# Second MoE in blocks of 512 tokens, one w_in chunk a step, in place of blocks of 256 and two chunks

## The chip, the core and the metric

The kernel runs on one core of one Trainium2 chip. The metric is the device time of one execution in microseconds (us). PE is TensorE (its weight loads are shown apart, as PEld), DVE is VectorE, ACT is ScalarE, POOL is GpSimd and SP is SyncE, which here only issues DMAs.

## The reference

Sliding-window attention feeds a bilinear MoE, and its result feeds a second MoE with a rational activation. The second MoE is what the change touches:

```
x = attention(q, k, v)                    # (2304, 512) after the heads are put together
x = ((x @ w1) * (x @ w2)) @ w3 @ w_out    # first MoE: 512 -> 1024 -> 1024 -> 512
h = x @ w_in                              # second MoE: 512 -> 2048
P = a[0] + a[1]*h + a[2]*h**2 + a[3]*h**3
Q = 1.0 + abs(b[0])*abs(h) + abs(b[1])*h**2
out = (P / (Q + 1e-06)) @ w_out           # 2048 -> 512
```

Inputs are float64 words that the kernel turns into fp32. To keep accuracy each operand of the large products is held as a high and a low part in fp32r, and a product is three matmuls: high by high, high by low, low by high (`SPLIT`).

## The kernel before

Phase 1 runs attention and the first MoE by a planner that orders its jobs. The first MoE works on chunks of 288 tokens (`TA`); its last chunk is finished inside phase 2 by `tail(n)`, n from 0 to 3.

Phase 2 is written out by hand, and each engine runs its instructions in the written order. The 2304 tokens are nine blocks of `TB` = 256. The 16 chunks of 128 hidden units are taken in four groups (`g`) of four. A step is one block and two chunks, so that a step's hidden tile is 128 x 512; there are 4 x 9 x 2 = 72 steps. What one step i writes, in this order:

- `hmm(i)` on PE: the hidden tile by 24 matmuls of 256 columns (two chunks, three products, four pieces of the contraction), into one of four PSUM banks (tags ab and px).
- `ins(i)`: ACT makes |h| (tile v), y and t, POOL multiplies y by v (L782), DVE makes the numerator in the hidden bank (L784, L785).
- `l4(i-4)` on PE: the output product of the step four before, 12 matmuls of 512 columns (L819) into accumulator banks, one for each 128 tokens. There are four of these banks (tags acc and sc), and a block of 256 tokens uses two over its two steps of a group.
- `split_g(i-1)`: ACT casts the quotient to its high part (L807), POOL subtracts for the low part (L808).
- `seed(i)` on ACT: Ln and Exp of the denominator (L791, L792); L791 waits for POOL's L782.
- `evict`: when a block's last `l4` of a group is written, its accumulators are copied to SBUF (ACT, L830, in group 0) or added to it (DVE, L832, later).
- `quotient(i)` on DVE (L797, L799, L801), and `weights(i)`, the load and the split of the next weights.
- `x_split` after steps 3, 6 and 9: a block's input is split, the high part by DVE (L740), the low part by POOL (L742). Five blocks are loaded and split in phase 1 (`NX1`), three in phase 2, and the last comes from `tail`.

At the start of phase 2, `tail(0)`, step 0, `tail(1)`, step 1, `tail(2)`, step 2 and `tail(3)` alternate, then the first four chunks of the second MoE's w_out are split (`b_split`: ACT L244, then POOL or DVE L248), and then steps 3, 4 and so on follow. Step 4 is the first with an `l4`.

Of the kernel before, what the change touches and what calls it, by code (L numbers as in the profile page):

```python
# [10 lines left out]
F32 = mybir.dt.float32  # L11
F32R = mybir.dt.float32r
# [6 lines left out]
P = 128  # L19
B, H, S, D = 4, 8, 576, 64  # L20
HP = H // 2
NT = B * S
# [158 lines left out]
class Kern:  # L181
# [308 lines left out]
    def phase1(self):  # L490
# [189 lines left out]
        done.eng = "DVE"  # L680
        for blk in range(NX1):
            ks = range(blk * TB // TA, ((blk + 1) * TB - 1) // TA + 1)
            ld = add("SP", 1.7, self.x_load, blk, after=[done] + [stored[k, n] for k in ks for n in range(KC)],
                     due=end - 30 + 5 * blk)
            add("DVE", 1.95, self.x_split, blk, after=[ld], due=end - 25 + 5 * blk, port=True)
        for f in range(FG):
            db = buf("dec0")
            pb = buf(f"p{f}")
# [39 lines left out]

    def x_load(self, blk):

        n = TB if blk < NB - 2 else TL
        x = self.XS[blk][:, 1].bitcast(F32)
        self.nc.sync.dma_start(out=x[:, :, 0:n], in_=self.x2d[:, :, blk * TB:blk * TB + n].rearrange(
            "c p t -> p c t"))

    def x_split(self, blk, lo_pool=False):
        nc = self.nc
        n = TB if blk < NB - 2 else TL
        hi, lo = self.XS[blk][:, 0, :, 0:n], self.XS[blk][:, 1, :, 0:n]
        nc.vector.tensor_copy(hi, lo.bitcast(F32))  # L740
        eng = nc.gpsimd if lo_pool else nc.vector
        eng.tensor_tensor(out=lo, in0=lo.bitcast(F32), in1=hi.bitcast(F32), op=ALU.subtract)  # L742

    def phase2(self, X, wk):
        nc, XS = self.nc, self.XS
        steps = [(g, blk, h) for g in range(NG) for blk in range(NB) for h in range(FG // 2)]
        PG = NB * FG // 2
        N = len(steps)
        hps, tt, yy, rr, gt, acc, adds = {}, {}, {}, {}, {}, {}, []
        self.nh = self.na = 0  # L750

# [4 lines left out]
        def accbank():  # L756
            self.na += 1
            return self.bank(("acc", "acc", "sc", "sc")[(self.na - 1) % 4])

        def buf(tag, bufs):  # L760
            return wk[tag].tile([P, 2 * TB], F32, tag=tag, bufs=bufs, name=tag)

        def hmm(i):
            g, blk, h = steps[i]
            t = hps[i] = hbank()
            for e in range(2):
                w = self.win[g * FG + 2 * h + e]
                n = 0
                for s in SPLIT:
                    for c in range(KC):  # L770
                        nc.tensor.matmul(t[:, e * TB:(e + 1) * TB], w[:, s[0], c * P:(c + 1) * P],  # L771
                                         XS[blk][:, s[1], c], start=n == 0, stop=n == 11)
                        n += 1

# [27 lines left out]
                                           op1=ALU.mult, reverse0=True)  # L802

        def split_g(i):
            u = tt.pop(i).rearrange("p (e t) -> p e t", e=2)
            t = gt[i] = self.gp.tile([P, 2, 2, TB], F32R, tag="g", bufs=5, name="gg")
            nc.scalar.copy(t[:, 0], u)  # L807
            nc.gpsimd.tensor_tensor(out=t[:, 1], in0=u, in1=t[:, 0].bitcast(F32), op=ALU.subtract)  # L808

        def l4(i):  # L810
            g, blk, h = steps[i]
            t = gt.pop(i)
            if h == 0:
                acc[g, blk] = [accbank() for _ in range(TB // P)]
            for e in range(2):
                w = self.wo2[g * FG + 2 * h + e]
                for tk in range(TB // P):
                    for s in SPLIT:
                        nc.tensor.matmul(acc[g, blk][tk], t[:, s[0], e, tk * P:(tk + 1) * P],  # L819
                                         w[:, s[1]], start=(h, e) == (0, 0) and s == (0, 0),  # L820
                                         stop=(h, e) == (FG // 2 - 1, 1) and s == (1, 0))
            if h == FG // 2 - 1:
                adds.extend((g, blk, tk) for tk in range(TB // P))

        def evict(on_act):
            if adds and on_act == (adds[0][0] == 0):
                g, blk, tk = adds.pop(0)
                a, x = acc[g, blk][tk], X[blk][:, tk * DM:(tk + 1) * DM]
                if g == 0:
                    nc.scalar.copy(x, a)  # L830
                else:
                    nc.vector.tensor_tensor(out=x, in0=a, in1=x, op=ALU.add)  # L832
                if g == NG - 1:
                    r = blk * TB + tk * P
                    nc.sync.dma_start(out=self.out[r:r + P, :], in_=x)

        def weights(i):
# [14 lines left out]
        def step(i):  # L852
            if i < N:
                hmm(i)
                ins(i)
            if i >= LAG:
                l4(i - LAG)
            if 1 <= i <= N:
                split_g(i - 1)
            if i < N:  # L860
                seed(i)
            evict(False)
            if i < N:
                quotient(i)
                weights(i)
            evict(False)
            evict(True)
            evict(True)
            for blk, k in X_SPLIT:
                if i == k:  # L870
                    self.x_split(blk, True)

        def tail(n):

            for e in range(2):
                self.l2(NA - 1, n, e)
            d = TA - TB
# [7 lines left out]
        for blk, _ in X_SPLIT:  # L885
            self.x_load(blk)
        for f in range(2):
            self.b_load(1, f)
# [11 lines left out]
    def run(self):  # L900
        with self.pool("cpool") as self.cpool, self.pool("decp") as self.decp, \
# [6 lines left out]

            def new_x(pool, blks):
                for n in blks:  # L910
                    self.XS[n] = pool.tile([P, 2, KC, TB], F32R, name=f"XS{n}")

# [6 lines left out]
            def attention_done():  # L919
                over.close()  # L920
                wk["r"] = right.enter_context(self.pool("b3", side="right"))
                new_x(wk["r"], range(NX1))

            self.attention_done = attention_done
            with self.pool("Q") as self.Q, self.pool("xs23") as self.xs23, self.pool("tp") as self.tp:
# [1 line left out]
                    self.phase1()  # L927
            with self.pool("b1") as b1:
                for n in range(NB):
                    X[n] = b1.tile([P, KC * TB], F32, name=f"X{n}")  # L930
                new_x(b1, range(NB - 1, NX1 - 1, -1))
# [61 lines left out]
```

## Time and profile before

| | us |
|---|---|
| median of 3 runs | 880.43 |
| lowest and highest | 877.05, 881.59 |
| the profiled execution, its time | 881.49 |
| the profiled execution, its span | 879.72 |

The span is the time from the first to the last instruction. The profile is of one execution, and the trace's times are counted from the span's start. Phase 2 takes the stretch from about 460 us to the end.

### The profile page before, as it was taken

How to read it: one execution, taken by the hardware profiler on the slowest of the kernel's cores; microseconds unless marked ns; L12 is line 12 of the kernel's file. 1: busy time of each engine (PE TensorE's matmuls, PEld its weight loads, DVE VectorE, ACT ScalarE, POOL GpSimd, SP SyncE). 2: the span in 40 equal slices, each digit the busy share in tenths (PEclk: the TensorE clock that was granted, in tenths of full speed). 3: DMA queues.
4: the chain of work that ended last, by engine and by line, in shares of the span. 5: the costliest groups of instructions: out<-in, count | busy, mean ns of one | idle time of the engine just before them, and what ended most of it. 6: DMA issues, size and time to landing. Idle time of an engine off the chain costs nothing.

```text
span 879.7 us, 16149 instructions
## 1 busy us (share of the span) xinstructions
PE 850.3 (97%) x5984; PEld 759.7 (86%) x5984; DVE 584.6 (66%) x1275; ACT 540.5 (61%) x1240; POOL 338.3 (38%) x316
## 2 busy tenths in 40 slices
PE   6989798999999999999999999999999999999998
PEld 3546598999998999989999889999999999999996
DVE  6999996677764212326125567779878877797775
ACT  5874564555465424542235578989877777787663
POOL 2220031332223221312122566676655655564442
PEclk9999999899999999999999999999999999999999
DMA  9776337576652202013111100010000100000112
GB/s 363 285 275 229 128 132 241 181 235 229 239 192 86 73 2 73 19 53 96 55 52 63 49 13 25 13 37 25 25 13 25 37 13 13 13 25 37 48 48 85
DMA packets 37710, 84.54 MB, mean 96 GB/s; under 512 B 4096, under 2 KB 11776, under 8 KB 37632
## 3 DMA queue, kind: packets, MB, share of 16 engines
q1 hardware_dynamic: 37632, 83.51, 27.8%
q8 instruction: 47, 0.77, 0.4%
q14 instruction: 31, 0.25, 0.1%
HBM read 66.26 MB, written 17.24 MB: 95 GB/s over the span
## 4 chain that ended last, share of the span: by engine, by line
PE 77%; DVE 7%; DMA 6%; ACT 5%; issue 3%; POOL 1%; SPq 0%; POOLq 0%; DVEq 0%; ACTq 0%
PE ab L437 20%; PE sc L819 11%; PE px L771 10%; PE acc L819 10%; PE ab L771 10%; PE acc L467 9%; DMA words<-moe_w_in 2%; PE sc L319 2%; PE px L384 2%; DMA words<-moe_w 2%; PE acc L417 2%; PE px L369 1%; DVE dec L226 1%; DMA qT<-q 1%; PE ab L417 1%
## 5 line engine op out<-in xcount | busy, mean ns | idle before, releaser
L437 PE MATMUL ab<-xs,w 128*128 128x288 f32 x1536 | 218.6, 302 | 6.1 <-ACT a_sb L443 2.7
L437 PEld LDWEIGHTS ab<-xs,w 128*128 128x128 f32 x1536 | 209.6, 191 | 12.3 <-ACT w L244 3.3
L782 POOL TENSOR_TENSOR y<-y,v 128x512 f32<-128x512 f32 x72 | 95.2, 1322 | 145.8 <-ACT y L781 144.0
L459 POOL TENSOR_TENSOR pp<-p,pp 128x288 fp32r<-128x288 f32 x64 | 54.0, 845 | 196.2 <-ACT pp L454 193.2
L362 POOL TENSOR_TENSOR pr<-pr,sm 96x384 f32<-96x384 f32 x64 | 55.2, 880 | 151.4 <-DVE sm L353 106.9
L467 PE MATMUL acc<-pp,w 128*128 128x288 f32 x768 | 111.2, 299 | 0.0
L771 PEld LDWEIGHTS px<-XS,w 128*128 128x128 f32 x864 | 106.8, 190 | 2.7 <-issue 0.2
L771 PEld LDWEIGHTS ab<-XS,w 128*128 128x128 f32 x864 | 106.9, 190 | 2.6
L771 PE MATMUL px<-XS,w 128*128 128x256 f32 x864 | 107.8, 281 | 0.0
L771 PE MATMUL ab<-XS,w 128*128 128x256 f32 x864 | 107.8, 281 | 0.0
L819 PE MATMUL acc<-w,gg 128*128 128x512 f32 x432 | 104.9, 391 | 1.4 <-POOL w L248 0.8
L819 PE MATMUL sc<-w,gg 128*128 128x512 f32 x432 | 104.7, 391 | 1.0 <-ACT X L830 1.0
L467 PEld LDWEIGHTS acc<-pp,w 128*128 128x128 f32 x768 | 103.5, 188 | 2.3
L808 POOL TENSOR_TENSOR gg<-t,gg 128x512 fp32r<-128x512 f32 x72 | 93.4, 1297 | 5.8 <-ACT gg L807 5.1
L819 PEld LDWEIGHTS acc<-w,gg 128*128 128x128 f32 x432 | 78.8, 188 | 16.9 <-POOL w L248 1.2
L819 PEld LDWEIGHTS sc<-w,gg 128*128 128x128 f32 x432 | 78.8, 188 | 16.3 <-ACT X L830 1.2
L346 ACT ACTIVATE pr<-pr,sm 96x128 f32<-96x128 f32 x192 | 74.7, 391 | 22.3 <-DVE sm L340 21.2
L447 DVE TENSOR_TENSOR p<-a_sb,ab 128x288 f32<-128x288 f32 x64 | 29.0, 452 | 88.7 <-PE ab L437 80.6
L799 DVE SCALAR_TENSOR_TENSOR v<-y,cs,r 128x512 f32<-128x512 f32 x72 | 77.1, 1071 | 0.0
L791 ACT ACTIVATE r<-y,cs 128x512 f32<-128x512 f32 x72 | 52.3, 727 | 27.2 <-POOL y L782 27.2
L218 ACT ACTIVATE dec<-words 128x512 f32<-128x512 f32 x72 | 47.6, 674 | 33.6 <-DMA words<-moe_w_in 11.3
L454 ACT CAST pp<-p 128x288 fp32r<-128x288 f32 x64 | 27.6, 432 | 56.1 <-DVE p L447 56.0
(77 smaller groups left out, 1199.4 us busy)
## 6 DMA issues: line engine op xcount, KB each, us to landing
words<-moe_w SPq DMA_DIRECT2D x32, 512.0 KB, 5.4
words<-moe_w_out SPq DMA_DIRECT2D x24, 512.0 KB, 4.5
words<-moe_w_in SPq DMA_DIRECT2D x16, 512.0 KB, 4.0
wd<-dec SPq DMA_DIRECT2D x32, 256.0 KB, 2.3
c<-wd SPq DMA_DIRECT2D x32, 256.0 KB, 2.7
vb<-v SPq DMA_DIRECT2D x16, 384.0 KB, 3.5
kT<-k SPq DMA_DIRECT2D x16, 304.0 KB, 4.7
qT<-q SPq DMA_DIRECT2D x16, 288.0 KB, 5.3
```

What stands on the lines that cost most here:

```text
L218: self.nc.scalar.activation(out=d.bitcast(F32), in_=s["words"].bitcast(F32)[:, :, 1], func=AF.Copy, scale=2.0 ** -112)
L346: self.nc.scalar.activation(out=pr[:, i], in_=pr[:, i], func=AF.Exp, scale=0.125, bias=sm[:, 1, i:i + 1], accum_out=sm[:, 2, i:i + 1])
L362: nc.gpsimd.tensor_tensor(out=pr[:, i], in0=pr[:, i], op=ALU.mult, in1=sm[:, 3, i].unsqueeze(2).to_broadcast([QT, 3, P]))
L437: self.nc.tensor.matmul(t[:, 0:TA], w[:, s[0], c * P:(c + 1) * P], xs[:, s[1], c], start=n == 0, stop=n == 11)
L459: eng.tensor_tensor(out=w[:, 1], in0=p, in1=w[:, 0].bitcast(F32), op=ALU.subtract)
L467: self.nc.tensor.matmul(acc[:, 0:TA], self.W3o[m][0][:, a, n * P:(n + 1) * P], self.p2[k, m // 2][:, c, m % 2], start=m == 0 and (a, c) == ...
L771: nc.tensor.matmul(t[:, e * TB:(e + 1) * TB], w[:, s[0], c * P:(c + 1) * P], XS[blk][:, s[1], c], start=n == 0, stop=n == 11)
L782: nc.gpsimd.tensor_tensor(out=w, in0=w, in1=v, op=ALU.mult)
L791: nc.scalar.activation(out=r, in_=yy[i][1], func=AF.Ln, bias=self.c1)
L799: nc.vector.scalar_tensor_tensor(out=v, in0=w, scalar=self.c1, in1=r, op0=ALU.add, op1=ALU.mult)
L808: nc.gpsimd.tensor_tensor(out=t[:, 1], in0=u, in1=t[:, 0].bitcast(F32), op=ALU.subtract)
L819: nc.tensor.matmul(acc[g, blk][tk], t[:, s[0], e, tk * P:(tk + 1) * P], w[:, s[1]], start=(h, e) == (0, 0) and s == (0, 0), stop=(h, e) == ...
```

## The change

`TB` becomes 512: four blocks of 512 tokens and one of 256 (`BLK`). In a block of 512 a step takes one chunk, so that the hidden tile is again 128 x 512, now by 12 matmuls of 512 columns; the block of 256 keeps two chunks a step. There are again 72 steps, and `l4` again has 12 matmuls of 512 columns, now over four accumulator banks for each block of 512. Phase 1 loads and splits two blocks of 512 rather than five of 256. A block's input is split in two halves. In phase 2 these halves are split after steps 2, 4, 6 and 8. `evict` is called up to four times a step on either engine: the copies on ACT now stand ahead of `seed` and behind it, and the additions on DVE ahead of `quotient`.

```diff
-TB = 256
-NB = NT // TB
-TL = NT - TA - (NB - 2) * TB
-NX1 = 5
+TB = 512
+NB = 5
+BLK = tuple((n * TB, min(TB, NT - n * TB)) for n in range(NB))
+NX1 = 2
+TL = NT - TA - BLK[NB - 2][0]
...
-X_SPLIT = ((5, 3), (6, 6), (7, 9))
+X_SPLIT = ((2, 0, 2), (2, 1, 4), (3, 0, 6), (3, 1, 8))
...
-    def x_split(self, blk, lo_pool=False):
+    def x_split(self, blk, i, lo_pool=False):
         nc = self.nc
-        n = TB if blk < NB - 2 else TL
-        hi, lo = self.XS[blk][:, 0, :, 0:n], self.XS[blk][:, 1, :, 0:n]
+        n = TL if blk == NB - 2 else TB
+        c = slice(i * KC // 2, (i + 1) * KC // 2)
+        hi, lo = self.XS[blk][:, 0, c, 0:n], self.XS[blk][:, 1, c, 0:n]
...
-        steps = [(g, blk, h) for g in range(NG) for blk in range(NB) for h in range(FG // 2)]
-        PG = NB * FG // 2
+
+        steps = [(g, blk, f) for g in range(NG) for blk in range(NB)
+                 for f in range(0, FG, TB // BLK[blk][1])]
...
-            for e in range(2):
-                w = self.win[g * FG + 2 * h + e]
+            nt = BLK[blk][1]
+            for e in range(TB // nt):
+                w = self.win[g * FG + f + e]
...
-                        nc.tensor.matmul(t[:, e * TB:(e + 1) * TB], w[:, s[0], c * P:(c + 1) * P],
+                        nc.tensor.matmul(t[:, e * nt:(e + 1) * nt], w[:, s[0], c * P:(c + 1) * P],
...
-            if h == 0:
-                acc[g, blk] = [accbank() for _ in range(TB // P)]
+            nt = BLK[blk][1]
+            if f == 0:
+                acc[g, blk] = [accbank() for _ in range(nt // P)]
...
+            evict(True)
+            evict(True)
             if i < N:
                 seed(i)
-            evict(False)
+            evict(True)
+            evict(True)
+            for _ in range(4):
+                evict(False)
             if i < N:
                 quotient(i)
                 weights(i)
-            evict(False)
-            evict(True)
-            evict(True)
-            for blk, k in X_SPLIT:
+            for blk, h, k in X_SPLIT:
                 if i == k:
-                    self.x_split(blk, True)
+                    self.x_split(blk, h, True)
```

PE, around steps 4 and 5, in the kernel before: XS is a block's input, w a weight chunk (w_in in the first kind of row, w_out in the second), gg the quotient's parts, and ab, px, acc and sc are bank tags.

```order
L771 MATMUL ab<-XS_4698,w 128x256 x24
L819 MATMUL acc<-w,gg 128x512 x12
L771 MATMUL ab<-XS_4698,w 128x256 x24
L819 MATMUL acc<-w,gg 128x512 x12
L771 MATMUL px<-XS_4699,w 128x256 x24
```

One block's output product takes acc only, and the next block's takes sc. The same engine in the changed kernel, from step 7 to step 9 (L778 is the hidden product, L828 the output product):

```order
L778 MATMUL px<-XS_4697,w 128x512 x12
L828 MATMUL acc<-w,gg 128x512 x6
L828 MATMUL sc<-w,gg 128x512 x6
L778 MATMUL ab<-XS_5375,w 128x512 x12
L828 MATMUL acc<-w,gg 128x512 x6
```

Each step's output product now takes all four banks, and the block that follows takes the same four.

POOL, where phase 2 begins, in the kernel before: y is the denominator's product, c and w are a loaded chunk and its two parts.

```order
L808 TENSOR_TENSOR gg<-t,gg 128x512
L248 TENSOR_TENSOR w<-c,w 128x512 x2
L782 TENSOR_TENSOR y<-y,v 128x512
L808 TENSOR_TENSOR gg<-t,gg 128x512
L742 TENSOR_TENSOR XS_5388<-XS_5388 128x1024
L782 TENSOR_TENSOR y<-y,v 128x512
```

The same place in the changed kernel (L746 is the subtraction of `x_split`, L249 that of `b_split`, L789 and L815 are y and gg):

```order
L815 TENSOR_TENSOR gg<-t,gg 128x512
L746 TENSOR_TENSOR XS_5375<-XS_5375 128x1024
L249 TENSOR_TENSOR w<-c,w 128x512 x2
L789 TENSOR_TENSOR y<-y,v 128x512
L815 TENSOR_TENSOR gg<-t,gg 128x512
L789 TENSOR_TENSOR y<-y,v 128x512
```

The first `x_split` has moved ahead of the two w_out chunks, from behind them.

ACT, steps 5 and 6, in the kernel before (v, y and t of `ins`, the cast gg, r of `seed`, a chunk of weights, then the copies of block 0's accumulators):

```order
L780 ACTIVATE v<-ab 128x512
L781 ACTIVATE y<-v,cs 128x512
L783 ACTIVATE t<-ab,cs 128x512
L807 CAST gg<-t 128x512
L791 ACTIVATE r<-y,cs 128x512
L792 ACTIVATE r<-r 128x512
L244 CAST w<-c 128x512
L830 COPY X_5376<-acc 128x512 x2
L780 ACTIVATE v<-px 128x512
```

In the changed kernel block 0's copies (now L839) stand in step 7:

```order
L787 ACTIVATE v<-px 128x512
L788 ACTIVATE y<-v,cs 128x512
L790 ACTIVATE t<-px,cs 128x512
L814 CAST gg<-t 128x512
L839 COPY X_5369<-acc 128x512 x2
L798 ACTIVATE r<-y,cs 128x512
L799 ACTIVATE r<-r 128x512
L839 COPY X_5369<-sc 128x512 x2
L787 ACTIVATE v<-ab 128x512
```

Block 0 ends two steps later than before, and its four copies stand two ahead of the step's Ln and Exp and two behind them.

## Rows read from the trace of the kernel before

**Rows 1.** The page: the span, and PE's busy time, share and instructions.

```profile
span 879.7 us, 16149 instructions
...
PE 850.3 (97%) x5984; PEld 759.7 (86%) x5984; DVE 584.6 (66%) x1275; ACT 540.5 (61%) x1240; POOL 338.3 (38%) x316
```

**Rows 2.** Groups by line and form: count, then busy us and mean ns.

```profile
L771 PE MATMUL px<-XS,w 128*128 128x256 f32 x864 | 107.8, 281 | 0.0
...
L819 PE MATMUL acc<-w,gg 128*128 128x512 f32 x432 | 104.9, 391 | 1.4 <-POOL w L248 0.8 <-ACT w L244 0.6
```

**Rows 3.** Timeline of PE, 448 to 548 us, and the last matmuls.

```profile
485.71 0.50 PE L819 MATMUL acc<-w,gg 128*128 128x512 f32 x1 [0.60 <-ACT w L244]
487.06 2.79 PE L819 MATMUL acc<-w,gg 128*128 128x512 f32 x11 [0.84 <-POOL w L248]
489.68 2.96 PE L771 MATMUL ab<-XS,w 128*128 128x256 f32 x24
492.49 2.91 PE L819 MATMUL acc<-w,gg 128*128 128x512 f32 x12
...
503.58 2.91 PE L819 MATMUL sc<-w,gg 128*128 128x512 f32 x12
...
521.49 3.02 PE L819 MATMUL sc<-w,gg 128*128 128x512 f32 x12 [1.04 <-ACT X L830]
...
535.59 3.04 PE L771 MATMUL ab<-XS,w 128*128 128x256 f32 x24
...
862.32 2.91 PE L819 MATMUL sc<-w,gg 128*128 128x512 f32 x12
```

**Rows 4.** Timeline of PE in the steady part, 640 to 663 us.

```profile
644.60 2.91 PE L819 MATMUL acc<-w,gg 128*128 128x512 f32 x12
647.35 3.04 PE L771 MATMUL ab<-XS,w 128*128 128x256 f32 x24
650.22 2.91 PE L819 MATMUL acc<-w,gg 128*128 128x512 f32 x12
```

**Rows 5.** Timeline of ACT, steps 3 to 7.

```profile
490.90 0.59 ACT L780 ACTIVATE v<-px 128x512 f32<-128x512 f32 x1
...
495.11 0.58 ACT L780 ACTIVATE v<-ab 128x512 f32<-128x512 f32 x1
...
497.41 0.62 ACT L807 CAST gg<-t 128x512 fp32r<-128x512 f32 x1 [0.20 <-DVE t L801]
501.73 0.73 ACT L791 ACTIVATE r<-y,cs 128x512 f32<-128x512 f32 x1 [3.71 <-POOL y L782]
...
503.03 0.58 ACT L780 ACTIVATE v<-ab 128x512 f32<-128x512 f32 x1
...
507.75 1.07 ACT L830 COPY X<-acc 128x512 f32<-128x512 f32 x2
508.71 0.61 ACT L780 ACTIVATE v<-px 128x512 f32<-128x512 f32 x1
...
512.94 0.58 ACT L780 ACTIVATE v<-px 128x512 f32<-128x512 f32 x1
```

**Rows 6.** Timeline of POOL, the first w_out chunk and the first x_split.

```profile
485.74 1.27 POOL L248 TENSOR_TENSOR w<-c,w 128x512 fp32r<-128x512 f32 x1 [3.49 <-ACT w L244]
...
498.06 2.40 POOL L742 TENSOR_TENSOR XS<-XS 128x1024 fp32r<-128x1024 f32 x1 [3.03 <-ACT gg L807]
```

**Rows 7.** Timeline of DVE, the end of tail(3) and the first x_split.

```profile
484.51 0.42 DVE L882 TENSOR_TENSOR XS<-acc,XS 128x256 fp32r<-128x256 f32 x1
...
497.29 0.69 DVE L740 CAST XS<-XS 128x1024 fp32r<-128x1024 f32 x1
```

**Rows 8.** Two stretches of phase 1: PE's busy us (count), then the granted clock.

```profile
149.00:154.00 5.00, 2.21 (x20) 0.91 0.59 225
154.00:160.00 6.00, 6.00 (x27) 0.51 0.54 186
```

**Rows 9.** Timeline of DVE in the steady part, 640 to 663 us.

```profile
653.96 0.68 DVE L832 TENSOR_TENSOR X<-acc,X 128x512 f32<-128x512 f32 x1
```

More of the change, by code (lines that the diff above doesn't have):

```diff
@@ L682, in phase1 @@
             ks = range(blk * TB // TA, ((blk + 1) * TB - 1) // TA + 1)
-            ld = add("SP", 1.7, self.x_load, blk, after=[done] + [stored[k, n] for k in ks for n in range(KC)],
-                     due=end - 30 + 5 * blk)
-            add("DVE", 1.95, self.x_split, blk, after=[ld], due=end - 25 + 5 * blk, port=True)
+            ld = add("SP", 3.4, self.x_load, blk, after=[done] + [stored[k, n] for k in ks for n in range(KC)],
+                     due=end - 30 + 12 * blk)
+            for i in range(2):
+                add("DVE", 1.95, self.x_split, blk, i, after=[ld], due=end - 25 + 12 * blk + 5 * i, port=True)
         for f in range(FG):
@@ L760, in buf @@
         def buf(tag, bufs):
[L761 removed]
+            return wk[tag].tile([P, TB], F32, tag=tag, bufs=bufs, name=tag)
         def hmm(i):
[L764 removed]
+            g, blk, f = steps[i]
             t = hps[i] = hbank()
[L766 to L767 removed]
+            nt = BLK[blk][1]
+            for e in range(TB // nt):
+                w = self.win[g * FG + f + e]
                 n = 0
@@ L810, in l4 @@
         def l4(i):
-            g, blk, h = steps[i]
+            g, blk, f = steps[i]
             t = gt.pop(i)
-            if h == 0:
-                acc[g, blk] = [accbank() for _ in range(TB // P)]
-            for e in range(2):
-                w = self.wo2[g * FG + 2 * h + e]
-                for tk in range(TB // P):
-                    for s in SPLIT:
[L819 to L823, printed above, removed]
+            nt = BLK[blk][1]
+            if f == 0:
+                acc[g, blk] = [accbank() for _ in range(nt // P)]
+            for e in range(TB // nt):
+                w = self.wo2[g * FG + f + e]
+                for tk in range(nt // P):
+                    j = e * nt + tk * P
+                    for s in SPLIT:
+                        nc.tensor.matmul(acc[g, blk][tk], t[:, s[0], j:j + P], w[:, s[1]],
+                                         start=f + e == 0 and s == (0, 0),
+                                         stop=f + e == FG - 1 and s == (1, 0))
+            if f + TB // nt == FG:
+                adds.extend((g, blk, tk) for tk in range(nt // P))
         def evict(on_act):
@@ L883, in tail @@
                                         op=ALU.subtract)
-        for blk, _ in X_SPLIT:
+        for blk in range(NX1, NB - 1):
             self.x_load(blk)
@@ L921, in attention_done @@
                 wk["r"] = right.enter_context(self.pool("b3", side="right"))
-                new_x(wk["r"], range(NX1))
+                new_x(wk["r"], (*range(NX1), NB - 1))
             self.attention_done = attention_done
@@ L929, in run @@
                 for n in range(NB):
-                    X[n] = b1.tile([P, KC * TB], F32, name=f"X{n}")
-                new_x(b1, range(NB - 1, NX1 - 1, -1))
+                    X[n] = b1.tile([P, BLK[n][1] // P * DM], F32, name=f"X{n}")
+                new_x(b1, range(NB - 2, NX1 - 1, -1))
                 wk["t"] = wk["v"] = wk["y"] = b1
```

18 lines of the change are left out of this document (10 added, 8 removed).

## The prediction

> **What bounds the kernel now.** I read the page first. PE is busy 850 of 880 us [rows 1], so a change is worth what it takes from PE's queue, less what it makes PE wait. Then I read PE's timeline through phase 2, for the price of a matmul and for PE's waits. A price is taken from starts, not from the printed durations, which overlap. A step's output product of 12 matmuls of 512 columns takes 2.75 us, 229 ns each (644.60 to 647.35) [rows 4]. The hidden product of 24 matmuls of 256 columns comes at two prices: 2.81 us, 117 ns each, for the five blocks that were split in phase 1 (489.68 to 492.49) [rows 3], and 2.87 us, 120 ns each, for the other four (647.35 to 650.22) [rows 4]. In the steady part nothing stands between these rows. PE waits at two places near the start of phase 2: some 1.4 us for the first w_out chunk before step 4's output product, and 1.0 us for ACT's copies before 521.49 [rows 3].
>
> Third, ACT's timeline at the same place. ACT starts v of step 7 at 512.94 [rows 5], although PE had finished step 7's hidden product at 503.58, where the output product of that step starts [rows 3]. ACT is thus 9.4 us late in step 7. The kernel pays little for it: PE may run ahead because `l4` works four steps behind, and two accumulator banks are free while the other two wait for their copies.
>
> **The change, part by part.**
>
> *Matmuls.* Of 1728 hidden matmuls of 256 columns (twice 864 [rows 2]), 64 steps' become 64 x 12 of 512 columns; 8 steps keep 24 of 256. No row shows w_in against a 512-column block. The nearest is the output product in the same phase, the same type and 512 columns: 229 ns. Two bounds: twice the dearer 256-column price is 239 ns, and the bare column time at the full clock (2.4 GHz, granted clock 1.00) is 213 ns, an estimate of what a matmul without any gap would take. I take 229, since it is the row of that very shape. A step's hidden product then takes 2.75 in place of 2.81 or 2.87 us. The elementwise work keeps its tiles of 128 x 512 and its 72 steps, so it costs the same.
>
> From step 13 on, where nothing waits any more, the sum is: before, from 535.59 (hidden product of step 13) to 862.32 (the last five output products) [rows 3] 326.7 us, for 59 hidden products and 58 output products. After: 51 x 2.745 + 8 x 2.81 + 58 x 2.745 = 321.7 us. **Gain 5.0 us.** What follows 862.32 is the same work and costs the same.
>
> *Phase 1* splits four halves of 128 x 1024 rather than five blocks of 128 x 1024; PE's order is unchanged there, and DVE has long waits for PE, so I put it at nothing (bounds: 0.7 us either way, one cast's time).
>
> *The first x_split goes ahead of the w_out split.* It now stands after step 2. Its cast takes DVE where `tail(3)`'s subtraction stood (484.51) [rows 7]; POOL starts 0.77 us behind a cast (497.29 to 498.06) [rows 6, 7], so at 485.2, and is held for 2.40 less an overlap of 0.05, to 487.57. POOL's half of the first w_out chunk, formerly at 485.74 [rows 6], starts there: 1.83 us later. PE's second output matmul, at 487.06 before, follows at 488.89, and step 5's hidden product at 491.51 rather than 489.68 [rows 3]. The buffer behind it is loaded again 1.83 us later, so ACT's v of step 3 moves from 490.90 to 492.73 [rows 5].
>
> *The copies of block 0 move from step 5 to step 7, and the next block needs the same banks.* This is the large term. Before, block 2 asked for block 0's banks in step 8, three steps after the copies stood on ACT. Now block 1's first output product, in step 8, asks for copies that stand on ACT in step 7. ACT's late time now counts in full.
>
> ACT's prices, from v to v: a plain step 4.21 (490.90 to 495.11) or 4.23 (508.71 to 512.94); a step after an `x_split` 7.92 (495.11 to 503.03), because POOL must finish the split before y, and L791 waits 3.71 us for y; a chunk of weights adds 5.68 - 4.23 - 0.96 = 0.49 (503.03 to 508.71, less the copies at 507.75) [rows 5]. `x_split` now follows steps 2, 4, 6 and 8. Hence v of step 4 at 492.73 + 4.21 = 496.94, of step 5 at 501.15, of step 6 at 501.15 + 7.92 + 0.49 = 509.56, of step 7 at 513.79. The first copy stands 2.92 behind v (497.41 + 0.62 - 495.11 [rows 5]), at 516.71. PE gets the bank some 0.62 after a copy starts (half of 1.07, and the signal), at 517.33.
>
> PE meanwhile: steps 5, 6 and 7 from 491.51 at 2 x 2.745 = 5.49 each, and step 8's hidden product to 510.72. **Wait 6.6 us.** Two banks' matmuls take PE to 518.70. The third copy stands behind Ln and Exp, and Ln waits for the split after step 6: 7.92 behind v, at 521.71, so PE goes on at 522.33. **Wait 3.6 us.** Step 9's hidden product starts at 523.70.
>
> ACT goes on: v of step 8 at 521.71 + 1.07 = 522.8, step 9 at 527.5 (with weights), step 10 at 535.4 (after the last split), step 11 at 539.6. The copies of block 1 start at 542.5 and, behind Ln and Exp, at 544.8. PE ends step 12's hidden product at 523.70 + 3 x 5.49 + 2.75 = 542.9 and waits 0.3, then 0.9 us. Step 13 starts at 546.8, against 535.59: **11.2 us late.** By then ACT follows PE directly, so the debt is paid once.
>
> *The clock.* PE idles longer than at any place of phase 2 before. In phase 1 PE was busy 2.21 us of 5, and in the next 6 us the granted clock is 0.51, the lower level, 1.2 GHz of 2.4 [rows 8]. If that happens around 517 to 524 us, PE loses about 2 us in the banks' matmuls and step 9; some 1.2 of it falls into the wait in step 12, which then disappears. I add 0.8. (The Trainium skill, "TensorE: Matmul & The Clock Gate", Part 1, also has PE fall to 1.2 GHz after idling; the trace agrees, with 0.51.)
>
> *Steady block ends.* In groups 1 to 3 DVE adds four banks, each 0.68. The first addition can start 3.74 us after the hidden product ends (653.96 less 650.22) [rows 4, 9], and then needs 0.68 and about 0.1 for the signal: the bank is free at 4.5. PE asks for it at 5.49, and both then go on at nearly the same pace, 0.68 a bank. The margin is 1.0 us at each of the block ends; cost nothing, unless DVE is that late.
>
> *Sum.* +11.2 + 0.8 - 5.0 = +7.0 us. On the profiled execution's own 881.49 that is 888.5. That execution lies 1.06 above the median of the runs, so I predict **887.4** for the median.
>
> **Rivals.** A change under 0.5%, 4.4 us, I call no change: 876.0 to 884.8.
>
> *The banks don't bind (faster).* If ACT reached block 0's copies before PE asks, the 10.2, 1.2 and 0.8 us go. Step 9 starts at 513.4, step 13 at 535.4, the gain of 5.0 stands: 875.2. It decides at v of step 7: 507.2 or earlier (510.72 - 0.62 - 2.92). In the kernel before, with one split fewer ahead of it, it is at 512.94, so this has little behind it. 9%.
>
> *The wide matmul is cheaper.* With 213 ns, 51 x 12 x 15.7 ns = 9.6 us more are won: 877.8, no change. Against it: the 512-column rows show 229. 12%. The Trainium skill, "TensorE: Matmul & The Clock Gate", section "Wait — 56ns, not 53.3ns?", gives 215.7 ns for back-to-back matmuls of 512 columns; by it the sum would be 879.3, and this trace's 229 ns don't agree.
>
> *The wide matmul wins nothing.* At 239 ns, 51 x 12 x 10 ns = 6.1 us are lost: 893.5. For it: the four later blocks already pay 120 ns for 256 columns, and two of the wide blocks are allocated where those were. 14%.
>
> *Block ends cost PE in the steady part too.* If DVE comes 1.5 us late at the 14 or so later block ends, each costs 0.5: 894.4. For it: only 1.0 us of margin. Against it: DVE is idle a third of the time [rows 1]. 12%.
>
> **How the numbers follow.** My forecast has 53%. The range goes from 878, the cheap matmul, to 896, the two dear cases; what it leaves out is the faster case and the sum of both dear ones. Faster 0.10; no change 0.17 (the cheap matmul and the lower edge of the forecast); slower 0.73.
>
> **What would show it.** Right: PE's largest wait in phase 2 is at step 8's output product, for ACT's copies, 5 to 8 us, with a second of 2 to 4 between its second and third bank; step 5's hidden product some 1.8 us later than before; hidden products of 2.75 us; no waits past step 13; PE's step 13 some 11 to 12 us later. The forecast is wrong if v of step 7 starts well before 513, if 12 wide matmuls take under 2.65 or over 2.85 us, or if waits for DVE's additions recur every four steps.

## The result, and the profile after

| | before | after |
|---|---|---|
| median of 6 runs each, taken side by side | 881.01 | 889.27 |
| lowest and highest | 877.05, 882.17 | 887.47, 891.55 |
| the profiled execution, its time | 881.49 | 888.94 |
| the profiled execution, its span | 879.72 | 887.16 |

The changed kernel is 1.0% slower: the ratio is 1.0102, with a 95% interval from 1.0076 to 1.0127. The forecast was 887.4 us in a range from 878 to 896, and slower with a chance of 0.73.

The page of the changed kernel, the engines (busy us, share of the span, instructions):

```profile
PE 849.9 (96%) x5216; PEld 724.7 (82%) x5216; DVE 574.6 (65%) x1274; ACT 542.6 (61%) x1240; POOL 341.2 (38%) x317
```

PE has 768 instructions fewer than before [rows 1], and nearly the same busy time (849.9 us, before 850.3). A busy share thus tells nothing of this change; starts do. PE's timeline of the changed kernel (start us, printed us, engine, line, operation, tiles, forms, count, and in brackets the idle time ahead with what ended it; L778 is the hidden product, L828 the output product), first where phase 2 begins, then a place in the second group, then the last output products:

```profile
486.49 0.50 PE L828 MATMUL acc<-w,gg 128*128 128x512 f32 x1 [1.22 <-ACT w L245]
489.52 2.50 PE L828 MATMUL acc<-w,gg 128*128 128x512 f32 x5 [2.53 <-POOL w L249]
491.82 2.77 PE L828 MATMUL sc<-w,gg 128*128 128x512 f32 x6
494.38 3.25 PE L778 MATMUL ab<-XS,w 128*128 128x512 f32 x12
...
511.33 2.88 PE L778 MATMUL ab<-XS,w 128*128 128x512 f32 x12
517.99 2.18 PE L828 MATMUL acc<-w,gg 128*128 128x512 f32 x6 [3.77 <-ACT X L839]
522.86 2.93 PE L828 MATMUL sc<-w,gg 128*128 128x512 f32 x6 [2.69 <-ACT X L839]
525.59 2.99 PE L778 MATMUL ab<-XS,w 128*128 128x512 f32 x12
...
547.53 2.89 PE L778 MATMUL ab<-XS,w 128*128 128x512 f32 x12
...
602.75 2.97 PE L778 MATMUL px<-XS,w 128*128 128x512 f32 x12
605.55 1.55 PE L828 MATMUL sc<-w,gg 128*128 128x512 f32 x6
...
619.43 2.88 PE L778 MATMUL px<-XS,w 128*128 128x512 f32 x12
622.15 1.52 PE L828 MATMUL sc<-w,gg 128*128 128x512 f32 x6
...
869.49 1.55 PE L828 MATMUL sc<-w,gg 128*128 128x512 f32 x6
```

From step 13 (547.53) to the last output products (869.49) it is 321.96 us, where it was 326.73 before [rows 3]: the wide matmul wins 4.8 us. But step 13 starts 11.94 us later than before (535.59 [rows 3]). That is where the time went (0.17 of it is a later start of phase 2). Step 5 is 4.70 us late already (494.38, before 489.68), and step 9 starts behind two waits for ACT's copies.

ACT's timeline of the changed kernel in the same stretch (L787 is v, L798 the Ln, L839 the copies out of the accumulator banks):

```profile
491.99 1.23 ACT L245 CAST w<-c 128x512 fp32r<-128x512 f32 x2 [5.03 <-DMA c<-wd]
493.12 0.59 ACT L787 ACTIVATE v<-px 128x512 f32<-128x512 f32 x1
...
509.95 0.59 ACT L787 ACTIVATE v<-px 128x512 f32<-128x512 f32 x1
...
514.54 0.58 ACT L787 ACTIVATE v<-px 128x512 f32<-128x512 f32 x1
...
517.36 1.07 ACT L839 COPY X<-acc 128x512 f32<-128x512 f32 x2
520.95 0.72 ACT L798 ACTIVATE r<-y,cs 128x512 f32<-128x512 f32 x1 [2.52 <-POOL y L789]
...
522.24 1.05 ACT L839 COPY X<-sc 128x512 f32<-128x512 f32 x2
```

These rows answer to [rows 5]. PE asks for the first bank when step 8's hidden product ends, at 511.33 + 2.72 = 514.05. The copy starts at 517.36, and PE goes on 0.63 later. The third copy (522.24) stands behind Ln (520.95), Ln behind POOL's y, and y behind the split on POOL, as POOL's rows show:

```profile
517.45 2.25 POOL L746 TENSOR_TENSOR XS<-XS 128x960 fp32r<-128x960 f32 x1 [2.74 <-ACT gg L814]
519.65 1.26 POOL L789 TENSOR_TENSOR y<-y,v 128x512 f32<-128x512 f32 x1
```

Two stretches of the changed kernel (PE's busy us and count, then PEld, DVE, ACT and POOL, then the granted clock of PE):

```profile
488.00:494.00 6.00, 4.48 (x11) 3.56 (x12) 1.10 (x2) 1.98 (x4) 2.74 (x2) 0.51 0.24 87
...
518.00:525.00 7.00, 4.31 (x11) 2.97 (x12) 2.85 (x4) 4.41 (x8) 4.35 (x4) 0.56 0.00 0
```

After both waits the granted clock is 0.51 and 0.56, so PE is for most of these stretches at its lower level, 1.2 GHz. Before, the clock granted in the same two stretches was 1.00.

POOL's timeline of the changed kernel, the first w_out chunk, which stands behind the first split, and then DVE's, the first additions at a block's end in the second group:

```profile
487.76 1.71 POOL L249 TENSOR_TENSOR w<-c,w 128x512 fp32r<-128x512 f32 x1
```

```profile
620.41 1.28 DVE L841 TENSOR_TENSOR X<-sc,X 128x512 f32<-128x512 f32 x2
```

### The profile page after: what moved, and what is told of

It reads as the page before. It is cut to its first block, busy times and chain, and to the rows that moved or that the text cites. A ratio compares the mean times of both kernels' runs of the same rounds, so it can differ in the third digit from the quotient of the medians.

```text
span 887.2 us, 14496 instructions
## 1 busy us (share of the span) xinstructions
PE 849.9 (96%) x5216; PEld 724.7 (82%) x5216; DVE 574.6 (65%) x1274; ACT 542.6 (61%) x1240; POOL 341.2 (38%) x317
## 4 chain that ended last, share of the span: by engine, by line
PE 78%; DVE 8%; ACT 4%; DMA 4%; issue 3%; POOL 2%; SPq 0%; POOLq 0%; DVEq 0%; ACTq 0%
PE ab L438 21%; PE sc L828 11%; PE acc L828 10%; PE px L778 10%; PE ab L778 10%; PE acc L468 7%; PE acc L418 2%; PE sc L320 2%; PE px L385 2%; DVE dec L227 2%; PE px L370 1%; DMA words<-moe_w_out 1%; PE ab L418 1%; DMA words<-moe_w_in 1%; ACT pr L347 1%
## 5 line engine op out<-in xcount | busy, mean ns | idle before, releaser
L789 POOL TENSOR_TENSOR y<-y,v 128x512 f32<-128x512 f32 x72 | 95.3, 1323 | 145.5 <-ACT y L788 144.3
L828 PE MATMUL acc<-w,gg 128*128 128x512 f32 x432 | 111.7, 395 | 7.5 <-ACT X L839 3.8
L828 PE MATMUL sc<-w,gg 128*128 128x512 f32 x432 | 112.1, 397 | 2.7 <-ACT X L839 2.7
L778 PE MATMUL ab<-XS,w 128*128 128x512 f32 (+1 forms) x480 | 105.8, 370 | 0.0
L778 PE MATMUL px<-XS,w 128*128 128x512 f32 (+1 forms) x480 | 105.4, 370 | 0.0
L828 PEld LDWEIGHTS acc<-w,gg 128*128 128x128 f32 x432 | 81.5, 190 | 26.1 <-ACT X L839 4.2
L828 PEld LDWEIGHTS sc<-w,gg 128*128 128x128 f32 x432 | 82.3, 192 | 21.3 <-ACT X L839 3.6
L778 PEld LDWEIGHTS ab<-XS,w 128*128 128x128 f32 x480 | 84.3, 189 | 16.6
L778 PEld LDWEIGHTS px<-XS,w 128*128 128x128 f32 x480 | 83.7, 188 | 16.2
L815 POOL TENSOR_TENSOR gg<-t,gg 128x512 fp32r<-128x512 f32 x72 | 93.4, 1297 | 7.8 <-ACT gg L814 7.2
L806 DVE SCALAR_TENSOR_TENSOR v<-y,cs,r 128x512 f32<-128x512 f32 x72 | 70.4, 978 | 0.0
L798 ACT ACTIVATE r<-y,cs 128x512 f32<-128x512 f32 x72 | 52.3, 727 | 24.0 <-POOL y L789 23.9
```

Of the source, the lines that this page charges most:

```text
L778: nc.tensor.matmul(t[:, e * nt:(e + 1) * nt], w[:, s[0], c * P:(c + 1) * P], XS[blk][:, s[1], c], start=n == 0, stop=n == 11)
L789: nc.gpsimd.tensor_tensor(out=w, in0=w, in1=v, op=ALU.mult)
L798: nc.scalar.activation(out=r, in_=yy[i][1], func=AF.Ln, bias=self.c1)
L806: nc.vector.scalar_tensor_tensor(out=v, in0=w, scalar=self.c1, in1=r, op0=ALU.add, op1=ALU.mult)
L828: nc.tensor.matmul(acc[g, blk][tk], t[:, s[0], j:j + P], w[:, s[1]], start=f + e == 0 and s == (0, 0), stop=f + e == FG - 1 and s == (1, 0))
```

## The experiments

Executions start phase 2 up to 9 us apart, because phase 1 varies. So places inside phase 2 are counted from step 0's hidden product of the same execution: 461.38 before and 461.55 after. Step 13 then stands at 74.2 before and 86.0 after. Times of before are medians of runs on the same chip, and "one run" means a single execution. The changed kernel was timed beside 881.01 alone, so where an edit of it is set against it by time, that is done by the ratio to before, 1.0102.

### What makes ACT late

**The low halves on DVE.** The subtraction of the four input splits in phase 2 moves from POOL to DVE, so that y no longer stands behind it.

```diff
-                    self.x_split(blk, h, True)
+                    self.x_split(blk, h, False)
```

> In the changed kernel the low part of the four input splits of phase 2 goes from POOL to DVE; all else stays. Theory (ACT's lateness at block 0's copies is made by the splits on POOL, which hold up y and so ACT's Ln): DVE does the same subtraction in 1.2 to 1.8 us in a stretch where it waits 3.8 us for ACT, so a step after a split costs ACT some 4.7 to 5.5 us in place of 7.9. v of step 7 starts near 511.6 in place of 514.5, the first copy near 514.5 and the third near 517, in place of 517.4 and 522.2. Step 9 starts 6 to 8 us earlier, and the time is 881 to 884. The wait for the first w_out chunk in step 4 stays, since the split still stands ahead of it, now on DVE. Rival (the copies themselves, or the four banks, cost it whatever ACT waits for): no change, 888 to 890.

884.98 us (881.91 to 888.12, 6 runs) against 879.63, a ratio of 1.0058 [1.0029, 1.0087]: about 4 us of the loss are gone, and the time lies 1 us above what was expected. ACT and PE of this kernel up to step 8:

```profile
510.75 0.62 ACT L814 CAST gg<-t 128x512 fp32r<-128x512 f32 x1 [2.56 <-DVE t L808]
...
515.39 1.07 ACT L839 COPY X<-acc 128x512 f32<-128x512 f32 x2
...
517.65 1.05 ACT L839 COPY X<-sc 128x512 f32<-128x512 f32 x2
```

```profile
516.02 1.77 PE L828 MATMUL acc<-w,gg 128*128 128x512 f32 x6 [3.08 <-ACT X L839]
518.27 2.81 PE L828 MATMUL sc<-w,gg 128*128 128x512 f32 x6 [0.48 <-ACT X L839]
```

The second pair of copies now comes 2.26 us behind the first rather than 4.88, and PE's second wait shrinks from 2.69 to 0.48. Step 13 stands at 82.0, 4.0 earlier than in the changed kernel. Most of the first wait stays (3.08, from 3.77): ACT is still late, now because the cast of the quotient waits 2.56 us for DVE.

**No low halves.** The same subtraction is left out of the kernel: the low part of blocks 2 and 3 stays the unsplit input.

```diff
-        eng = nc.gpsimd if lo_pool else nc.vector
-        eng.tensor_tensor(out=lo, in0=lo.bitcast(F32), in1=hi.bitcast(F32), op=ALU.subtract)
+        if not lo_pool:
+            nc.vector.tensor_tensor(out=lo, in0=lo.bitcast(F32), in1=hi.bitcast(F32), op=ALU.subtract)
```

> In the changed kernel the subtraction for the low part of the phase 2 input splits is left out (blocks 2 and 3 use the raw input as their low part); the casts stay. It shows the whole price of the splits on POOL. Theory: ACT reaches v of step 7 near 509, the first copy near 512, PE waits some 3 us in step 8 and 1 us more ahead of the third bank, and step 13 starts 8 to 10 us earlier than in the changed kernel: 879 to 881. What is left of the waits then comes from the w_out chunks in step 3 and 4. Rival (the price is that of the four banks alone): less than 2 us won, over 887.

One run: 882.17 against 879.63, 1 us above what was expected. Step 13 (540.75, step 0 at 464.04) stands at 76.7, against 86.0 in the changed kernel: these four subtractions account for 9.3 of its 11.8 us. PE's first wait for the copies in step 8 (the second is 0.59), and step 13:

```profile
515.24 1.66 PE L828 MATMUL acc<-w,gg 128*128 128x512 f32 x6 [1.12 <-ACT X L839]
...
540.75 2.88 PE L778 MATMUL ab<-XS,w 128*128 128x512 f32 x12
```

**The first split a step later.** Only the order changes: the first half is split after step 3, and so no longer ahead of the w_out split.

```diff
-X_SPLIT = ((2, 0, 2), (2, 1, 4), (3, 0, 6), (3, 1, 8))
+X_SPLIT = ((2, 0, 3), (2, 1, 4), (3, 0, 6), (3, 1, 8))
```

> In the changed kernel the first half's split goes from behind step 2 to behind step 3, so that it no longer stands ahead of the w_out chunks. Theory (the waits are one debt of ACT, paid where PE needs the copies): PE's wait in step 4 falls by some 2 us and the lower clock there is gone, but v of step 7 starts near 515.8, 1 us later than in the changed kernel, and step 8's waits grow to match: 888 to 891, no gain. Rival (the waits add up, each with its own cost): step 4's wait and its lower clock are worth 4 us, 884 to 886.

891.21 us (889.32 to 892.33, 4 runs) against 879.63, a ratio of 1.0132 [1.0106, 1.0158]. Step 5 is on time again, 28.3 behind step 0 as before, and the clock stays at 1.00 in step 4. Yet step 13 stands at 87.7, later than in the changed kernel. PE of this kernel, step 8's output product:

```profile
518.37 2.93 PE L828 MATMUL acc<-w,gg 128*128 128x512 f32 x6 [9.35 <-ACT X L839]
```

PE comes to step 8 earlier and waits longer. (The copy also comes later, 57.5 behind step 0 rather than 55.8: the splits after steps 3 and 4 make ACT wait 3.71 and 3.69 for y.) PE goes on when ACT's copy is there, whenever it came, so what PE loses in step 4 is no part of the sum in the changed kernel: it lies under the wait for ACT.

**The w_out chunks loaded early.** The first wait in ACT's rows of the changed kernel is for a DMA: 5.03 us for `c`, the third w_out chunk, whose buffer comes free late. Here all four chunks are loaded ahead of phase 2, two of them into buffers of their own.

```diff
-    def b_load(self, kind, f):
-        raw = self.decp.tile([P, DM], F32, tag="dec", bufs=2, name="c")
+    def b_load(self, kind, f, pool=None):
+        raw = (pool or self.decp).tile([P, DM], F32, tag="dec", bufs=2, name="c")
...
-        for f in range(2):
-            self.b_load(1, f)
+        for f in range(FG):
+            self.b_load(1, f, wk["v"] if f > 1 else None)
...
-            if f + 2 < FG:
-                self.b_load(1, f + 2)
```

> The changed kernel with all four w_out chunks of the first group loaded into buffers of their own ahead of phase 2. Theory (what makes PE wait in step 8 is how late ACT is, whatever made it late): v of step 7 starts about 4.3 us earlier relative to step 0, the waits for the copies in step 8 shrink by as much, step 13 stands 81 to 82 us behind step 0 in place of 86.0, and the time is 884 to 886 us. Rival (ACT's lateness up to step 4 is absorbed before step 7, where the splits set the pace): step 13 stands at 86, and the time at 888 to 889 us.

One run: 886.03 against 880.11. Step 13 stands at 82.55. PE of this kernel at step 8:

```profile
515.04 1.65 PE L828 MATMUL acc<-w,gg 128*128 128x512 f32 x6 [1.16 <-ACT X L839]
519.92 1.65 PE L828 MATMUL sc<-w,gg 128*128 128x512 f32 x6 [3.23 <-ACT X L839]
```

v of step 7 (at 511.59, step 0 at 462.06) is 49.5 behind step 0, against 53.0 in the changed kernel, and the first wait falls from 3.77 to 1.16. The second, which is set by the split on POOL, stays. So ACT's lateness from the DMA and that from the splits add up: without the DMA's part step 13 is 3.4 earlier.

### Whether it is the banks

**The split order in the kernel before.** The kernel before keeps its blocks of 256, and its three splits move to steps 2, 4 and 6.

```diff
-X_SPLIT = ((5, 3), (6, 6), (7, 9))
+X_SPLIT = ((5, 2), (6, 4), (7, 6))
```

> The kernel before, with its three input splits of phase 2 after steps 2, 4 and 6 in place of 3, 6 and 9, so that they press on ACT as early as in the changed kernel, while a block still takes two accumulator banks. Theory (the price is that the four banks leave ACT's lateness no room): step 4's wait grows as in the changed kernel, with the lower clock there, so that step 13 is 3 to 5 us later than in the kernel before; ACT is as late as in the changed kernel, v of step 7 near 516, but PE doesn't wait for block 0's copies in step 8, since they stand on ACT two steps before: 883 to 886. Rival (the early splits alone cost it, whatever the banks): step 13 is 11 us later, over 890.

884.16 us (879.56 to 887.02, 10 runs) against 880.66, a ratio of 1.0032 [1.0007, 1.0058]. Step 13 is 2.6 us later than before, less than expected. ACT is here as late as in the changed kernel: v of step 7 stands at 518.39, 54.0 behind step 0. But in step 8 PE asks, at 516.05, for two banks that ACT began to copy at 513.21, and doesn't wait; it loses time in step 4 alone. PE, then ACT's copies:

```profile
492.38 4.39 PE L819 MATMUL acc<-w,gg 128*128 128x512 f32 x11 [2.53 <-POOL w L248]
496.61 2.97 PE L771 MATMUL ab<-XS,w 128*128 128x256 f32 x24
...
516.05 2.91 PE L819 MATMUL acc<-w,gg 128*128 128x512 f32 x12
```

```profile
513.21 1.06 ACT L830 COPY X<-acc 128x512 f32<-128x512 f32 x2
```

With two banks a block the same lateness of ACT costs nothing at step 8; with four it costs the waits of 3.77 and 2.69.

**The additions behind the quotient.** The additions of the later groups move behind DVE's quotient and the weights, whose three instructions make them some 2 us later (0.76, 0.74 and 0.69), to see whether the steady block ends have the margin of 1.0 us that was worked out.

```diff
-            for _ in range(4):
-                evict(False)
             if i < N:
                 quotient(i)
                 weights(i)
+            for _ in range(4):
+                evict(False)
```

> In the changed kernel DVE's up to four additions into the output stand behind the quotient of the step, in place of ahead of it. It tests the steady margin of 1.0 us at the block ends. Theory: the first addition then starts 6.6 us behind the end of the step's hidden product in place of 3.74, so its bank is free at 7.4, and PE, which asks at 5.5, waits 1.9 us at each of 11 or 12 block ends of groups 1 to 3: 908 to 913, all of it in PE's waits for DVE. Rival (PE has more room than that, since output products lie four steps behind): 887 to 891.

One run: 924.87 against 879.63, more than expected. PE now waits at the block ends of groups 1 to 3, thirteen times between 1.20 and 2.79 us, 25.8 us in all. Four of these waits are for the high part of a later quotient, which now stands behind the additions:

```profile
675.00 1.62 PE L828 MATMUL sc<-w,gg 128*128 128x512 f32 x6 [1.74 <-DVE X L841]
700.14 4.37 PE L828 MATMUL sc<-w,gg 128*128 128x512 f32 x12 [2.67 <-ACT gg L814]
```

The second row's 12 matmuls print 4.37 us, because the clock falls behind the wait (0.72 granted from 700 to 706). Step 13 to the last output products takes 35 us more than in the changed kernel: the 25.8 us of waits, and what the lower clock behind some of them costs. The margin is small, and the changed kernel just keeps it.

### What a wide matmul costs

**Wide blocks, narrow matmuls.** The changed kernel with each hidden product of 512 columns as two of 256.

```diff
+                for j in range(0, nt, 256):
...
-                        nc.tensor.matmul(t[:, e * nt:(e + 1) * nt], w[:, s[0], c * P:(c + 1) * P],
-                                         XS[blk][:, s[1], c], start=n == 0, stop=n == 11)
+                            nc.tensor.matmul(t[:, e * nt + j:e * nt + j + 256],
+                                             w[:, s[0], c * P:(c + 1) * P],
+                                             XS[blk][:, s[1], c, j:j + 256], start=n == 0, stop=n == 11)
```

> The changed kernel with each hidden matmul of 512 columns made as two of 256, one after the other through the 12 products, so that all is as changed but the matmul's width. Theory (the width gains what the rows showed): the steps of blocks 0 and 1 stay at 2.81 us, those of blocks 2 and 3 go from 2.72 to 2.87: from step 13 to the last output products 326 to 327 us in place of 322.0, 893 to 895 in all. Rival (the gain from step 13 on has another source, the schedule): 322, and 889.

One run: 894.47 against 880.66. From step 13 (548.52) to the last output products (875.01) it is 326.49 us, where it was 326.73 before the change. So the gain is the width's: the blocks of 512 alone bring next to nothing.

```profile
548.52 3.04 PE L779 MATMUL ab<-XS,w 128*128 128x256 f32 x24
...
875.01 1.55 PE L830 MATMUL sc<-w,gg 128*128 128x512 f32 x6
```

**Aligned blocks.** The changed kernel has two prices of a wide matmul. Blocks 0 and 1, whose input starts 32 bytes beside a multiple of 64, take 2.80 us for 12 (602.75 to 605.55 above); blocks 2 and 3, which start on a multiple, 2.72 (619.43 to 622.15). A pad of 32 bytes moves the first two onto a multiple, and the block of 256 with them.

```diff
+                wk["r"].tile([P, 8], F32, name="pad")
```

> The changed kernel with 32 bytes more in the pool that holds the inputs of blocks 0 and 1, so that they start at a multiple of 64 bytes, as those of blocks 2 and 3 do; they started 32 bytes off. Theory A (a start off by 32 bytes makes the wide matmul 234 ns in place of 227, and the output product of such a step 2.757 us in place of 2.72): every step of blocks 0 and 1 loses 0.12 us, 2.9 us from step 13 on; in the first steps PE waits for ACT anyway; 885 to 887. Theory B (the difference belongs to another pool, or to the place in the sequence): no change, 888 to 890.

887.54 us, the median of 9 runs, against 880.66, a ratio of 1.0078 [1.0053, 1.0104]. (One of the nine took 3604.4 us, which nothing in the traces explains.) From step 13 on all wide hidden products now take 2.72 us, and step 13 (547.20) to the last output products (866.85) is 319.65, 2.3 us less than in the changed kernel. The trace shows this gain; by the runs, 1.0078 can't be told from 1.0102. PE in the second group, a step of block 1 and the block of 256:

```profile
607.40 2.88 PE L778 MATMUL ab<-XS,w 128*128 128x512 f32 x12
610.12 1.52 PE L828 MATMUL sc<-w,gg 128*128 128x512 f32 x6
...
661.80 3.04 PE L778 MATMUL px<-XS,w 128*128 128x256 f32 x24
664.67 0.63 PE L828 MATMUL sc<-w,gg 128*128 128x512 f32 x2
```

The block of 256 went the other way: 2.87 (661.80 to 664.67), where it was 2.80 or 2.81 off the multiple.

**The kernel before, blocks 5 to 8 off the multiple.** If that holds, the two prices of [rows 3] and [rows 4] are a matter of where a block starts.

```diff
+                b1.tile([P, 8], F32, name="pad")
```

> The kernel before with a pad of 32 bytes ahead of the input buffers that phase 2 allocates, so that blocks 5 to 8 start 32 bytes beside a multiple of 64, as blocks 0 to 4 do. Theory (a moving operand of 256 columns is read faster from such a start): the hidden products of steps 40 to 71 take 2.80 in place of 2.87 us, step 13 to the last output products takes 324.4 us in place of 326.7, and the time is about 878 us. Rival (the two prices come from the blocks' numbers or ages, not from the start): 326.7 us and no change. Other rival (starts on a multiple of 64 are better, as with 512 columns): it cannot become better, and stays or is slower.

(Steps 40 to 71 are not these blocks: blocks 5 to 8 have eight steps in each of the four groups.) 878.34 us (874.12 to 882.26, 10 runs) against 880.11, a ratio of 0.9981 [0.9959, 1.0003]. PE of this kernel in the steady part:

```profile
646.90 2.96 PE L771 MATMUL px<-XS,w 128*128 128x256 f32 x24
649.70 2.91 PE L819 MATMUL sc<-w,gg 128*128 128x512 f32 x12
```

From step 13 on all hidden products but one now take 2.80 or 2.81, and step 13 (530.03) to the last output products (854.93) is 324.90, 1.8 us less. The trace shows the gain; the runs can't tell it from none.

### Whether the gain can be had without the loss

**All three repairs.** The changed kernel with the splits on DVE, the w_out chunks loaded early and the aligned blocks (edits as above).

> The changed kernel with three edits: the phase 2 input splits wholly on DVE, the 32 bytes of padding, and w_out chunks 2 and 3 of the first group loaded into buffers of their own at the start of phase 2, so that ACT doesn't wait 5 us for them ahead of step 3. Theory (the loss is ACT's debt at the start, and the four-bank blocks cost nothing once ACT is on time): v of step 7 near 508, block 0's copies near 510.5, about when PE asks; step 13 some 73 us behind step 0 in place of 86.0, the stretch from there to the last output products 319 in place of 322: 870 to 875, faster than both kernels. Rival (four-bank blocks cost PE a wait at every block end whenever ACT or DVE copies): step 13 at 78 or more, 878 and over.

879.91 us (877.47 to 883.12, 12 runs) against 880.66, a ratio of 0.9986 [0.9967, 1.0005]: no change, and far from what was expected. Step 8 no longer waits, and step 13 to the end is 319.65 us, but step 13 stands at 78.7, 4.5 later than before. ACT and PE of this kernel where phase 2 begins:

```profile
490.76 0.18 ACT L892 CAST XS<-acc 128x32 fp32r<-128x32 f32 x1 [4.14 <-DVE XS L893]
```

```profile
491.52 0.50 PE L828 MATMUL acc<-w,gg 128*128 128x512 f32 x1 [2.71 <-ACT w L245]
492.87 2.50 PE L828 MATMUL acc<-w,gg 128*128 128x512 f32 x5 [0.85 <-POOL w L249]
...
497.73 3.54 PE L778 MATMUL ab<-XS,w 128*128 128x512 f32 x12
```

The split on DVE now stands ahead of `tail(3)` (L893), for which ACT waits, and PE for ACT's w_out half. The clock falls behind that wait (0.57 granted from 494 to 500), so 11 matmuls take 4.86 us (492.87 to 497.73). In step 12 PE waits another 0.88 and 0.59 for the copies. What the wait in step 8 had covered is now paid. The time is the one that the rival gave, but not for its reason: behind step 13 PE waits nowhere.

**Later splits as well.** The last edit was meant to take that loss away.

```diff
-X_SPLIT = ((2, 0, 2), (2, 1, 4), (3, 0, 6), (3, 1, 8))
+X_SPLIT = ((2, 0, 3), (2, 1, 4), (3, 0, 8), (3, 1, 10))
```

> The kernel of e8_all with its input splits behind steps 3, 4, 8 and 10 instead of 2, 4, 6 and 8. Theory (order on ACT and DVE around the first block end is all that is left of the loss): the first w_out half no longer stands behind a split, so step 5's hidden product is again 28.3 us behind step 0 (before: 28.3; e8_all: 32.4), step 8 still has no wait for the copies, step 13 stands 75 to 76 us behind step 0 (before: 74.2; e8_all: 78.7), the last output products about 395 us (before: 400.9; e8_all: 398.4), and the time is 874 to 878 us. Rival (ACT's lateness is a sum that any order pays): the splits behind steps 3 and 4 stand next to each other, v of step 7 comes as late as in e4, the wait returns in step 8 with 2 us or more, and the time is 879 us or more.

880.49 us (875.55 to 884.45, 12 runs) against 880.11, a ratio of 1.0008 [0.9986, 1.003]. Step 5 stands at 28.4, as the theory has it, but the wait in step 8 is back and the time is the rival's: step 13 stands at 80.7. PE of this kernel:

```profile
510.31 2.59 PE L828 MATMUL acc<-w,gg 128*128 128x512 f32 x6 [2.97 <-ACT X L839]
...
532.60 1.20 PE L778 MATMUL ab<-XS,w 128*128 128x512 f32 x4 [0.87 <-DVE XS L744]
```

PE comes to step 8 earlier than with the three repairs alone (44.7 behind step 0 rather than 49.4), but the first copy, with two splits in a row ahead of it, hardly does (49.9 rather than 50.5). (v of step 7 is not as late as the rival had it: 47.1 behind step 0, and 54.7 with the first split a step later.) The last split, after step 10, is late for step 12, which reads it. Every order tried here pays somewhere.

**The w_out chunks early in the kernel before** (the edit as in the changed kernel).

> The kernel before with all four w_out chunks of the first group loaded into buffers of their own ahead of phase 2, so that no half of a chunk on ACT waits for a DMA. Theory (ACT's lateness in steps 3 to 7 begins with that wait): v of step 3 starts 4 to 5 us earlier, the waits of 1.0 and 0.3 us in step 9 go, the gain is 1 to 1.5 us, 878.5 to 880 us. Rival: the cost is elsewhere, no change.

880.50 us (877.75 to 882.45, 10 runs) against 880.11, a ratio of 1.001 [0.9991, 1.0028]. In the trace v of step 7 comes 3.3 us earlier, the wait of 1.04 for the copies [rows 3] is gone (it stood in step 10, not 9), and step 13 stands at 73.0 in place of 74.2; a gain of 1.2 us is less than the runs can tell.

## Why the prediction was right

*The sum.* +7.0 us was forecast and the spans differ by 7.4 (887.16 less 879.72). Step 13 was forecast at 546.8 and 0.8 for the clock, 547.6; it is at 547.53, with the later start of 0.17 in it. From there to the last output products 321.7 was forecast and 321.96 measured. The last 0.3 lies behind them: 17.67 us are left there, 17.40 before. The medians differ by 8.3.

*The wide matmul.* 2.745 us for 12 was taken from the output product. No step has this price: of the 51 wide hidden products from step 13 on, 24 take 2.80 or 2.81 and 27 take 2.72, a mean of 2.76 (the output products now take 2.74 in the mean). The nearest row was a lucky choice, in that two blocks lie on either side of it. The narrow matmuls (326.49) show that the gain is the width's.

*The copies and the banks.* The mechanism holds. v of steps 3, 6 and 7 was forecast at 492.73, 509.56 and 513.79, and is at 493.12, 509.95 and 514.54. The copies were forecast at 516.71 and 521.71, and are at 517.36 and 522.24. Taking the split's subtraction away takes 9.3 us off step 13, and the same lateness with two banks a block costs nothing in step 8.

*What failed: when PE comes to step 8.* "Wait 6.6 us" and "wait 3.6 us" are 3.77 and 2.69 in the trace (the first is 3.94 by starts, 514.05 to 517.99). The largest wait was said to be 5 to 8, which it missed. PE asks at 514.05 and not at 510.72, mostly because the term of 1.83 for the first split was too small: step 5 is 4.70 late. (Of the other 0.46, 0.29 is the lower clock again, in step 5's hidden product, which takes 3.09 rather than 2.80; what is left is the wide steps of blocks 0 and 1.) The 2.87 between 1.83 and 4.70 have two parts. POOL's half of the first w_out chunk started 0.19 later than forecast (phase 2 starts 0.17 later; the prediction also has 485.2 where 484.51 + 0.77 is 485.28) and took 1.71 rather than 1.27: 0.63. Here DVE's half of the chunk starts first, at 486.99; before, POOL's did, at 485.74, and DVE's at 486.21. Then 11 matmuls took 4.86 us (489.52 to 494.38) rather than 2.62, since the clock fell behind the wait: 2.24. The forecast looked for the lower clock in step 8 alone. Little of it moved the sum, because ACT's copies set when step 9 starts. The split after step 3 shows it: without the loss of step 4, PE waits 9.35 in step 8.

*The clock in step 8.* 0.8 was forecast, as 2 us less what step 12's wait would cover. The second pair of banks takes 2.73 (522.86 to 525.59) in place of 1.36, so 1.4 were lost; the copy came 0.5 later than forecast, and step 12's waits of 0.3 and 0.9 are gone. From step 9 to step 13 it is 21.94 in place of the 23.1 forecast. These make up the 0.7 between 547.53 and 546.8. (The Trainium skill, "TensorE: Matmul & The Clock Gate", section "Wait — 56ns, not 53.3ns?", gives 426.7 ns for a cold matmul of 512 columns. The trace agrees: at the lower clock in step 4 six take 491.82 to 494.38, 427 ns each.)

*Steady block ends.* A margin of 1.0 us was worked out. In the second group the first addition ends at 620.41 + 0.68 = 621.09, and PE asks at 622.15, 1.06 later. No wait recurs. Moved 2 us later, the additions cost 35 us in all.

*The rivals.* That the banks don't bind asked for v of step 7 at 507.2, which it missed by 7 us. A wide matmul of 213 or 239 ns didn't come; 227 and 234 did.

## What to carry to other kernels

Before a tile is made larger, count the accumulator banks that one tile holds: when the next tile needs the same ones, the queue that empties them may no longer be late, and any lateness that it carries into that place, here from splits and a DMA that stand ahead on other engines, is paid in full. A loss ahead of such a wait is covered by it, and comes back when the wait is taken away: mending one place (step 8) uncovered the next (step 4), and three mends together brought only what the change had lost. Read starts, not busy shares: PE was as busy after as before.

## What the runs showed of the hardware

The start of the moving operand has a price. 24 matmuls of 256 columns take 2.80 us from a start 32 bytes beside a multiple of 64, and 2.87 from a multiple; 12 of 512 columns take 2.80 and 2.72, the other way round. A pad of 32 bytes alone moved 512 columns from 2.80 to 2.72, and 256 columns from 2.81 to 2.87 in one kernel and from 2.87 to 2.80 in another. Why the two widths differ in sign stays open, and no other starts were tried.

The same DVE instruction has two prices, by what POOL does. In the kernel with the low halves on DVE, the subtraction of 128 x 1024 first runs while POOL is idle, then beside POOL's own subtractions (504.36 to 505.95, and from 506.25):

```profile
485.49 1.23 DVE L746 TENSOR_TENSOR XS<-XS 128x1024 fp32r<-128x1024 f32 x1
...
504.82 2.21 DVE L746 TENSOR_TENSOR XS<-XS 128x1024 fp32r<-128x1024 f32 x1
```

The Trainium skill, "SBUF — State Buffer", section "Who interferes with whom", has DVE instructions with two inputs in SBUF and GpSimd's reads share a port, with the later one blocked. The trace agrees in kind, with 2.21 against 1.23. Moving a split from POOL to DVE thus doesn't take POOL off DVE's path.
